# Attention and a gated mixer in one kernel: ScalarE units of two PSUM banks, spread weight loads, and an order planned with other durations

## The chip, the cores and the metric

The kernel runs on one core of a Trainium2 chip. The metric is the device time of one execution in microseconds (us); the time before is the median of three runs, 762.45 us (760.06 to 764.45). One further execution was profiled; where a single operation, a wait or a sum is spoken of, it is from that one.

## The reference

Two blocks read the same input x (2048 tokens, 512 wide, bfloat16), and a gate mixes them. Block A is attention with 32 heads of 16; block B is a small mixer with token shifts and a second MLP of width 1792.

```python
g = _sigmoid((x * gate_w).sum(-1, keepdims=True))
# block A
q, k, v = heads(x @ wqkv)                       # 32 heads of 16
p = softmax(einsum("bhqd,bhkd->bhqk", q, k) * 16 ** -0.5)
a = merge(einsum("bhqk,bhkd->bhqd", p, v)) @ wo
# block B
h = gelu(layernorm(x) @ w1)                     # its four quarters moved by 1, -1, 2, -2 tokens
x1 = x + shifted(h) @ w2
b = x1 + gelu(layernorm(x1) @ w3) @ w4
return g * a + (1 - g) * b
```

## The kernel before

**Score tiles.** Attention is cut into 32 rounds: four chunks of 512 queries (`c`), four groups of eight heads (`G`), and the two parities of heads (`p`). A round has 64 score tiles: 16 key tiles of 128 (`kt`) for four heads (`i`), each head on its own 32 rows of TensorE. In all there are 2048 score matmuls (`qk_op`, L1293), each 128 keys by 512 queries, each filling one of the eight PSUM banks. The planner counts its progress in these tiles.

**Two ways to the exponential.** `issue_act` gives two or three neighbouring banks to ScalarE as one unit: a single `Exp` instruction over all of them (L1388) writes `pa_all`. `issue_dve` gives a tile to VectorE instead: a multiply and add into 16-bit integers, which read as bfloat16 approximate the exponential (L1418, the first step, into `PD`). Two such tiles make a pair, and `close_pair` makes three shifted copies of the pair, by VectorE (L1456) or GpSimd (L1458). A ScalarE tile needs one matmul with V afterwards (`take_pv`, L1510), a VectorE tile needs four, one for each copy, which average the error away.

**TensorE's two tilings.** Score matmuls use four row tiles of 32 rows. All others that matter use four column tiles of 32 columns: the matmuls with V, and the weight matmuls of the projections and MLPs, which `gen` records (L975). So TensorE changes between groups of score matmuls and stretches of column passes. A pass here is one matmul on each of the four column tiles.

**Layer steps in between.** `mlp1` and `mlp2` are the mixer's two MLPs. `normalise` makes `xn` (L1142) of a chunk, writes it to DRAM, and reads it back transposed as `xnT`. The matmuls with `w1`, `w2`, `w3` and `w4` come from `gen` with a planned place (`at`) and a due place (`due`), both in score tiles. Five Gelu instructions on ScalarE (one at L1182, four at L1213) take a whole chunk or all of them, each between two loads of the activation table. At a round's end `finish_round` divides by the sums, through several small transfers.

**The order.** Nothing of the order is left to a scheduler of the framework. `Sim` plays the engines in Python while the kernel is built: each job has an engine, a planned duration (`hold`), a delay until its result can be used (`lat`), a priority and the buffers it takes. `pe_pick` decides what TensorE gets next, ahead of all a unit for ScalarE where the banks allow it; `try_engine` picks the job of lowest priority number of the other four queues. What the play starts first is issued first, engine by engine, and the chip then follows that order with its own durations. Where TensorE has nothing in the play for 250 ns, `filler` issues idle matmuls on zeros (L1819).

**The knobs.** `BASE` and `STEPS` set some 30 numbers of these decisions, and `STEPS` may change them at every 8 score tiles (`SEG = 8`). The ones that this text needs: `CAP2` and `CAP3` are the most banks that ScalarE's units may hold when a unit of two or of three banks is to be added (0 means never); `P1_PRIO` and `S_PRIO` are the priorities of VectorE's first step and of its copies, against 0.35 of `xn`; `GP2` and `GP3` share the copies out between VectorE and GpSimd; `DVE_STOP` and `DVE_WAIT` limit VectorE's tiles.

**Durations that the planner uses before.** A unit of w banks on ScalarE takes

```python
hold = 0.833 * 512 * w + 67.0
```

a weight load lands 6.0 us after its issue whatever its size, and a copy on GpSimd can begin when no other copy through the port it shares with VectorE is planned to run:

```python
if j.port and self.lock > self.t or j.acq and any(not self.fits(b) for b in j.acq):
    continue
```

The four loads of `w3` may be issued from score tile 450 of the planner's places on (`P_LD[0]`), the four of `w4` from 888 (`P_LD[1]`).

Of the kernel before, what the change touches and what calls it, by code (L numbers as in the profile page):

```python
# [97 lines left out]
class Job:  # L98
    __slots__ = ("eng", "hold", "lat", "deps", "prio", "fn", "acq", "frees", "at", "done", "start", "seq", "ready", "name", "port", "watch", "deps_tiles")

    def __init__(self, eng, hold, lat, deps, fn, prio=5, acq=(), frees=(), at=0, name="", port=False):
        self.port = port
        self.eng, self.hold, self.lat, self.deps, self.fn = eng, hold, lat, list(deps), fn
        self.prio, self.acq, self.frees, self.at = prio, list(acq), list(frees), at
        self.done = self.start = None
        self.seq = 0
        self.ready = None
        self.name = name
        self.watch = []

# [41 lines left out]
class Sim:  # L152
# [4 lines left out]
    def __init__(self, slots):  # L157
# [13 lines left out]
        self.lock = 0.0  # L171
        self.pending = 0
# [109 lines left out]
    def try_engine(self, e):  # L282
# [17 lines left out]
        j = best[1]  # L300
# [9 lines left out]
        if j.port:  # L310
            self.lock = self.t + j.hold
        self.busy[e] += j.hold
# [3 lines left out]
        self.push(self.t + j.hold + j.lat, lambda: self.finish_job(j))  # L316
# [60 lines left out]
def kernel(  # L377
# [14 lines left out]
    nc = tc.nc  # L392
# [60 lines left out]
    STEPS = {  # L453
        0: dict(DVE_STOP=8, SL0=165, AHEAD2=16, PV_IDLE=0.117, MAXU=4, LIMD=4, LIMA=2),
        1: dict(DVE_STOP=6, DVE_WAIT=1, AHEAD=16, PV_IDLE=0.5, MAXU=3, AT_SH=69, LIMD=3, LIMA=3),
        2: dict(P1_PRIO=0.743, GP2=0.5, DVE_STOP_L=16, DVE_WAIT=3, AHEAD=3, PV_IDLE=0.731, PRESS=15, DUE_SH=16, CAP2=6,
            RES=1, JOIN=1),
        3: dict(P1_PRIO=0.414, S_PRIO=0.3, DVE_STOP=13, DVE_STOP_L=14, EARLY=64, AHEAD=9, AHEAD2=24, PV_FULL=0.947,
            PRESS=18, CAP2=5, CAP3=6, RES=0),
        5: dict(S_PRIO=0.38, DVE_STOP=8, DVE_ALONE=-158, EARLY=99, AHEAD=3, PV_FULL=0.813, MAXU=9, ROT=1, AT_SH=96,  # L460
            HOLE=2),
        6: dict(MAXU=2),
        7: dict(GP2=0.315, URG_L=18, DVE_ALONE=2, AHEAD=9, PRESS=26, MAXU=3, CAP3=5),
        8: dict(URG_L=12, AHEAD=12, PV_FULL=0.916, PRESS=18, MAXU=4, AT_SH=69, HOLE=7, ACC2=1),
        9: dict(P1_PRIO=0.743, S_PRIO=0.625, EARLY=64, AHEAD=9, AHEAD2=13, PV_FULL=0.947, PV_IDLE=0.117, MAXU=5, ROT=3,
            HOLE=2, CAP3=6),
        10: dict(AHEAD=12, AHEAD2=24, LIMD=2),
        11: dict(URG_L=18),
        12: dict(P1_PRIO=0.279, GP2=0.655, URG_L=12, EARLY=99, AHEAD=9, AHEAD2=13, PV_FULL=0.916, MAXU=3, ROT=0, HOLE=3,
            LIMD=3, ACC2=0),  # L470
        13: dict(P1_PRIO=0.55, GP2=0.315, EARLY=64, IDLE_NS=700, DVE_WAIT=4, AHEAD2=5, MAXU=4, HOLE=7, MAXG=2),
        14: dict(P1_PRIO=0.743, URG_L=18, IDLE_NS=537, DVE_WAIT=3, AHEAD=12, AHEAD2=24, PV_FULL=0.947, MAXU=5, ROT=3,
            HOLE=2, MAXG=1, LIMD=2, ACC2=1),
        15: dict(DVE_WAIT=2),
        16: dict(URG_L=12, DVE_WAIT=3, AHEAD=9, HOLE=0, LIMD=3),
        17: dict(P1_PRIO=0.279, GP3=1, HOLE=2, MAXG=2),
        18: dict(P1_PRIO=0.743, GP3=0.967, EARLY=99, SL0=45, IDLE_NS=374, PD_LOW=3, AHEAD2=5, PV_FULL=0.916, HOLE=7,
            MAXG=1, CAP3=0, ACC2=0),
        19: dict(DVE_ALONE=-158, EARLY=64, SL1=0, IDLE_NS=459, AHEAD2=24, PV_IDLE=0.5, ROT=0),
        20: dict(URG=8, URG_L=18, SL1=60, IDLE_NS=374, PD_LOW=1, PV_FULL=0.97, PV_IDLE=0.117, HOLE=2),  # L480
        21: dict(URG=5, URG_L=12, SL1=0, IDLE_NS=459, PD_LOW=3, PV_FULL=0.916, PV_IDLE=0.5, HOLE=7),
        22: dict(HOLE=3),
        23: dict(DVE_STOP_L=12, HOLE=7),
        25: dict(DVE_STOP_L=14, URG=8, DVE_ALONE=2, IDLE_NS=864, PD_LOW=1, PA_LOW=3, AHEAD2=13, ROT=3, AT_SH=96, CAP2=6,
            LIMD=4, JOIN=0),
        26: dict(DVE_STOP=4, URG=5, URG_L=18, SL1=60, IDLE_NS=700, PD_LOW=3, PA_LOW=0, DVE_WAIT=4, AHEAD2=24,
            PV_IDLE=0.117, AT_SH=69, CAP2=5, LIMD=3, JOIN=1),
        27: dict(GP3=1, DVE_STOP=8, URG=8, EARLY=99, SL0=100, SL1=0, PD_LOW=2, DVE_WAIT=3, AHEAD=7, PV_FULL=0.947,
            PV_IDLE=0.5, HOLE=2, LIMA=2),
        28: dict(URG_L=12, SL0=45, IDLE_NS=374, AHEAD=9, DUE_SH=-6, HOLE=7, LIMA=3),  # L490
        29: dict(P1_PRIO=0.136, GP3=0.967, EARLY=64, IDLE_NS=864, AHEAD2=13, PV_FULL=0.916, PV_IDLE=0.731, DUE_SH=16,
            AT_SH=96, CAP2=6, LIMD=4, JOIN=0),
        30: dict(P1_PRIO=0.743, S_PRIO=0.178, GP2=1, DVE_STOP_L=16, URG=11, IDLE_NS=374, AHEAD2=24, PV_IDLE=0.5, ROT=0,
            AT_SH=69, CAP2=4, ACC2=1, JOIN=1),
        31: dict(S_PRIO=0.625, DVE_STOP_L=14, EARLY=99, PV_IDLE=0.731, ROT=3, CAP2=5, ACC2=0, JOIN=0),
        32: dict(DVE_STOP_L=16, EARLY=64, IDLE_NS=459, PA_LOW=1, PV_FULL=0.947, PV_IDLE=0.5, ROT=0, LIMA=4),
        33: dict(S_PRIO=0.178, DVE_STOP_L=7, URG=3, IDLE_NS=374, PA_LOW=0, AHEAD=12, PV_FULL=0.916, PRESS=11, ROT=2,
            AT_SH=118, ACC2=1, LIMA=3, JOIN=1),
        34: dict(S_PRIO=0.625, DVE_STOP_L=14, URG=11, IDLE_NS=864, PD_LOW=3, AHEAD=9, AHEAD2=9, PV_IDLE=0.117, PRESS=18,
            ROT=0, AT_SH=69, ACC2=0, JOIN=0),  # L500
        35: dict(SL1=60),
        36: dict(P1_PRIO=0.414, SL1=0, ACC2=1),
        37: dict(P1_PRIO=0.743, ACC2=0),
        38: dict(DVE_STOP_L=16, DVE_ALONE=-158, IDLE_NS=459, PD_LOW=2, PA_LOW=1, AHEAD2=24, PV_FULL=0.947, PRESS=57,
            MAXU=3, CAP3=5, LIMA=4),
        39: dict(P1_PRIO=0.55, S_PRIO=0.214, DVE_STOP_L=14, URG=2, DVE_ALONE=2, SL0=0, PD_LOW=3, AHEAD=5, PV_FULL=0.916,
            PRESS=18, MAXU=2, CAP2=4, CAP3=0, ACC2=1, LIMA=2, JOIN=1),
        40: dict(P1_PRIO=0.743, S_PRIO=0.625, URG=11, DVE_ALONE=-81, SL0=45, PD_LOW=2, AHEAD=9, PV_IDLE=0.5, PRESS=11,
            MAXU=5, ROT=1, ACC2=0, LIMA=4, JOIN=0),
        41: dict(SL0=165),  # L510
        42: dict(S_PRIO=0.214, GP3=0.8, SL0=45, AHEAD=7, PV_IDLE=0.117, PRESS=43, MAXU=4),
        43: dict(DVE_STOP_L=7, HOLE=3, CAP3=6),
        44: dict(SL1=60),
        45: dict(S_PRIO=0.178, DVE_STOP=6, DVE_STOP_L=12, DVE_ALONE=2, SL0=0, SL1=0, IDLE_NS=864, PV_FULL=0.947,
            PRESS=26, HOLE=2, CAP3=0, JOIN=1),
        46: dict(IDLE_NS=537, MAXG=2),
        49: dict(IDLE_NS=459, DUE_SH=32, MAXG=1),
        50: dict(JOIN=0),
        51: dict(S_PRIO=0.3, IDLE_NS=537, JOIN=1),
        52: dict(S_PRIO=0.178, IDLE_NS=459, MAXU=5, DUE_SH=16),  # L520
        53: dict(IDLE_NS=864, MAXU=4),
        54: dict(IDLE_NS=459, DUE_SH=32, LIMA=2),
        55: dict(PD_LOW=3, LIMA=4),
        56: dict(DVE_ALONE=138, PD_LOW=2, PA_LOW=0, JOIN=0),
        57: dict(DVE_STOP=4, DVE_STOP_L=14, URG=8, DVE_ALONE=362, EARLY=99, PD_LOW=3, PA_LOW=1, PV_FULL=0.97, DUE_SH=16,
            MAXG=2, ACC2=1),
        59: dict(DVE_STOP=6, DVE_STOP_L=12, URG=11, DVE_ALONE=2, EARLY=64, PD_LOW=2, PV_FULL=0.947, MAXU=5, MAXG=1,
            ACC2=0, JOIN=1),
        60: dict(DVE_STOP=4, DVE_STOP_L=14, URG=8, DVE_ALONE=362, EARLY=99, PD_LOW=3, PV_FULL=0.97, MAXU=4, ROT=2,
            MAXG=2, CAP2=6, CAP3=5, ACC2=1),  # L530
        61: dict(S_PRIO=0.625, GP3=0.967, DVE_STOP=13, DVE_STOP_L=16, PRESS=11, MAXU=7, HOLE=0, CAP3=0),
        62: dict(DVE_STOP=4, IDLE_NS=537, PV_FULL=0.916, PRESS=26, HOLE=3, MAXG=1),
# [1386 lines left out]
```

## Time and profile before

| what | value |
|---|---|
| median of three runs | 762.45 us |
| profiled execution | 761.38 us, span of its instructions 759.4 us |
| ScalarE busy | 735.6 us, 744 instructions |
| TensorE busy (matmuls) | 746.4 us, 9545 matmuls recorded |
| VectorE busy | 704.9 us, 1428 instructions |
| GpSimd busy | 460.4 us, 458 instructions |
| ScalarE's exponentials | 669 of two banks, 50 of three |
| transfers | 34.57 MB, 46 GB/s on average |

Busy time is the time in which an engine had at least one instruction running. Matmuls and ScalarE's instructions overlap with their neighbours, so the mean duration of one is longer than the spacing between two of them. Score tiles can be read off the trace by counting matmuls of L1293: number 1024 starts 380.6 us into the span, number 1152 at 424.7.

### The profile page before, as it was taken

The numbers are of one execution on the slowest core, as the hardware profiler recorded it, in microseconds if no ns is written. First come the engines' busy times: TensorE is split into PE (matmuls) and PEld (weight loads), VectorE is DVE, ScalarE is ACT, GpSimd is POOL, SyncE is SP. The second block draws the span as 40 slices with busy tenths as digits, with TensorE's granted clock in tenths as the row PEclk, the third lists the DMA queues.
The fourth block names the chain that finished last, engine by engine and source line by source line (L and its number), as shares of the span: only waits on it lengthen the run. The fifth ranks groups of instructions, "written<-read, shape, count | busy, mean of one in ns | idle before, by whom it ended". The sixth has DMA issues, their size and how long they took to land.

```text
span 759.4 us, 23495 instructions
## 1 busy us (share of the span) xinstructions
PE 746.4 (98%) x9545; PEld 218.2 (29%) x9545; DVE 704.9 (93%) x1428; ACT 735.6 (97%) x744; POOL 460.4 (61%) x458
## 2 busy tenths in 40 slices
PE   9999999999999999999999999999999999999997
PEld 5343222222322222223222222422223222222332
DVE  6999899999999999999998999898999999999966
ACT  6999999999999999999998999999999999999995
POOL 2334476776785456775645767465466577767732
PEclk9999999999999999999999999999999999999999
DMA  9433211231001320042101000202000001000001
GB/s 189 150 87 58 53 47 33 48 100 65 21 6 48 79 68 13 15 133 65 38 15 33 27 20 21 47 11 58 23 27 19 15 17 28 26 27 21 20 16 34
DMA packets 67091, 34.57 MB, mean 46 GB/s; under 512 B 46748, under 2 KB 62380, under 8 KB 66984
## 3 DMA queue, kind: packets, MB, share of 16 engines
q1 hardware_dynamic: 66040, 32.56, 17.6%
q8 instruction: 74, 1.21, 0.7%
q10 hardware_dynamic: 944, 0.52, 0.2%
q14 instruction: 33, 0.27, 0.1%
HBM read 17.40 MB, written 6.81 MB: 32 GB/s over the span
## 4 chain that ended last, share of the span: by engine, by line
PE 72%; ACT 10%; DVE 9%; issue 3%; DMA 2%; POOL 2%; SPq 1%; POOLq 0%; DVEq 0%; ACTq 0%
PE banks L1510 25%; PE banks L1293 25%; PE banks L975 21%; ACT pa_all L1388 10%; DVE PD L1418 4%; DVE PD L1456 3%; POOL PD L1458 2%; DMA oD<-oT 1%; DMA pk<-den 1%; DMA xn_dram<-xn 1%; PE banks L954 0%; PE banks L1840 0%; SPq L1550 0%; POOL oT L1546 0%; PE banks L996 0%
## 5 line engine op out<-in xcount | busy, mean ns | idle before, releaser
L1388 ACT ACTIVATE pa_all<-banks 128x1024 bf16<-128x1024 f32 x719 | 685.7, 1137 | 9.8 <-PE banks L1293 7.9
L1458 POOL TENSOR_SCALAR PD<-PD 128x1024 uint16<-128x1024 uint16 x396 | 407.7, 1051 | 255.0 <-DVE PD L1456 117.8
L1418 DVE TENSOR_SCALAR PD<-banks 128x512 uint16<-128x512 f32 x554 | 366.3, 685 | 27.9 <-PE banks L1293 24.1
L1510 PE MATMUL banks<-PD,V 128*17 128x512 bf16 (+1 forms) x2240 | 300.2, 382 | 3.3 <-DVE PD L1456 1.5
L1293 PE MATMUL banks<-q,kT 32*128 32x512 bf16 x2048 | 288.8, 384 | 2.5 <-ACT pa_all L1388 1.3
L1510 PE MATMUL banks<-pa_all,V 128*17 128x512 bf16 (+1 forms) x1488 | 269.3, 381 | 0.0
L1456 DVE TENSOR_SCALAR PD<-PD 128x1024 uint16<-128x1024 uint16 x444 | 192.0, 476 | 1.4
L1293 PEld LDWEIGHTS <-kT 32*128 32x128 bf16 x2048 | 72.5, 91 | 313.9 <-ACT pa_all L1388 296.0
L1510 PEld LDWEIGHTS <-V 128*17 128x17 bf16 (+1 forms) x3728 | 72.5, 88 | 122.5 <-issue 104.3
L975 PE MATMUL banks<-xnT,w 128*32 128x512 bf16 x1152 | 95.6, 383 | 0.4 <-DVE PD L1418 0.2
L975 PE MATMUL banks<-w,hT 128*32 128x512 bf16 x704 | 59.6, 382 | 0.0
L975 PEld LDWEIGHTS <-w 128*32 128x32 bf16 x1920 | 43.6, 95 | 45.6 <-issue 27.4
L1546 POOL TENSOR_TENSOR oT<-accsb,bcs 128x512 bf16<-128x512 f32 x31 | 39.5, 1275 | 25.2 <-DVE PD L1456 16.0
L975 PE MATMUL banks<-w,hB 128*32 128x512 bf16 x448 | 43.0, 383 | 0.0
L975 PE MATMUL banks<-w,w 128*32 128x256 bf16 (+1 forms) x768 | 41.3, 311 | 0.0
L975 PE MATMUL banks<-wo,oD 128*32 128x512 bf16 x224 | 29.9, 383 | 1.2 <-DMA oD<-oT 1.1
L1530 DVE COPY accsb<-banks 128x512 f32<-128x512 f32 x31 | 21.1, 679 | 3.6 <-PE banks L1510 3.0
L975 PE MATMUL banks<-w,wq 128*32 128x512 bf16 x256 | 22.8, 383 | 0.3 <-ACT w L1006 0.3
L975 PEld LDWEIGHTS <-hT 128*32 128x32 bf16 x704 | 16.6, 95 | 18.9 <-issue 12.1
L1122 DVE BATCH_NORM_STATS2 st<-x_sb 128x6 f32<-128x512 bf16 x32 | 21.6, 683 | 0.1
L1212 DVE CAST hB<-banks 128x512 bf16<-128x512 f32 x28 | 18.9, 680 | 1.5 <-PE banks L975 1.4
L1212 DVE CAST hT<-banks 128x512 bf16<-128x512 f32 x28 | 18.8, 680 | 0.8 <-PE banks L975 0.7
(90 smaller groups left out, 253.9 us busy)
## 6 DMA issues: line engine op xcount, KB each, us to landing
bcs<-rr SPq DMA_DIRECT2D x124, 64.0 KB
xn_dram<-xn SPq DMA_DIRECT2D x32, 128.0 KB
w<-in_B_w_dram SPq DMA_DIRECT2D x5, 512.0 KB
oD<-oT SPq DMA_DIRECT2D x124, 16.0 KB
w<-in_B_w_dram SPq DMA_DIRECT2D x4, 448.0 KB
out_dram<-ot SPq DMA_DIRECT2D x14, 128.0 KB
x_sb<-in_A_x_dram SPq DMA_DIRECT2D x3, 512.0 KB
w<-in_A_wqkv_dram SPq DMA_DIRECT2D x2, 256.0 KB
```

Source lines behind the costliest of these rows:

```text
L975: units.append([Op("col", j, lambda j=j, lf=lf, rf=rf, n0=n0, n1=n1, st=st, sp=sp: nc.tensor.matmul(get()[32 * j:32 * j + 32, n0:n1], lhsT ...
L1122: a = dve(600, deps, lambda: nc.vector.bn_stats(out=sb.slot[:], in_=x_sb[:, t, :]), prio=6, at=at, acq=[sb])
L1212: pre.append(evac(g, PSUM_NS, lambda ps, m=m: nc.vector.tensor_copy(out=h2()[:, m, :], in_=ps[:])))
L1293: o = Op("row", i, lambda: nc.tensor.matmul(dst(), lhsT=kT[G][32 * i:32 * i + 32, kt * P:(kt + 1) * P], rhs=qbuf[G, c].slot[32 * i:32 * i ...
L1388: job = act(hold, ops, lambda: nc.scalar.activation(out=pa_all[:, pb.cut(), :], in_=unit()[:, rb.cut(), :], func=ACT.Exp, scale=0.25), acq ...
L1418: return nc.vector.tensor_scalar(out=pr["buf"].slot[:].rearrange("p (b c) -> p b c", c=512)[:, h0:h0 + w, :], in0=unit()[:, rb.cut(), :], ...
L1456: return nc.vector.tensor_scalar(out=d[k][:, 0:w], in0=d[0][:, 0:w], scalar1=float(SHIFT * k), scalar2=None, op0=ALU.add)
L1458: return nc.gpsimd.tensor_scalar(out=d[k][:, 0:w], in0=d[0 if both else 2][:, 0:w], scalar1=1.0, scalar2=float(SHIFT * (k if both else 1)) ...
L1510: return nc.tensor.matmul(one(accs[r])[32 * i:32 * i + n, :], lhsT=lhs(n), rhs=rhs(), start=st and not edge, stop=True, tile_position=(0, ...
L1530: e = dve(PSUM_NS, round_ops[r], lambda: nc.vector.tensor_copy(out=ab.slot[:], in_=one(accs[r])), acq=[ab], prio=0, frees=[accs[r], Call(a ...
L1546: n = gp(1250, d3, lambda: nc.gpsimd.tensor_tensor(out=ob.slot[:], in0=ab.slot[:], in1=bb.slot[:], op=ALU.mult), acq=[ob], frees=[ab, bb], ...
```

## The change

ScalarE's units have two banks throughout: `CAP3` is 0 everywhere, and `CAP2` is 6, or 5 for a stretch. A new knob, `GATE`, lets units be issued only while ScalarE's units hold no more than that many banks. The planner's durations are others: ScalarE's fixed part is 55 ns, weight loads take a time that goes by their size through a common queue, other transfers on that queue land no earlier than it allows, and GpSimd's copies wait in the play until VectorE's last port operation has ended and its result has landed. The loads of `w3` and of `w4` are released 20 score tiles apart from each other. `STEPS` is another table throughout. The operations that make up one ScalarE unit of two banks, one VectorE tile or one weight matmul are the same as before; how many of each there are, and in which order they stand, follows from the play. Lines after L920 or so have lower numbers in the changed kernel, most of them by 72 (L1388 becomes L1316, L1819 becomes L1747).

```diff
 def try_engine(self, e):
 ...
-            if j.port and self.lock > self.t or j.acq and any(not self.fits(b) for b in j.acq):
+            if j.port and (self.lock > self.t or e == "POOL" and self.dve_lock > self.t) or j.acq and any(not self.fits(b) for b in j.acq):
                 continue
 ...
         if j.port:
             self.lock = self.t + j.hold
+            if e == "DVE":
+                self.dve_lock = self.t + j.hold + j.lat
 ...
-        self.push(self.t + j.hold + j.lat, lambda: self.finish_job(j))
+        end = self.t + j.hold + j.lat
+        if e == "SP" and j.hold > 1.5:
+            if j.size:
+                self.queue = max(self.queue, self.t + j.hold) + j.size / 185.0
+            end = max(end, self.queue + 1500.0)
+        self.push(end, lambda: self.finish_job(j))

 BASE
-        ROT=2, DUE_SH=-14, AT_SH=0, HOLE=7, MAXG=1, CAP2=4, CAP3=0, LIMD=3, RES=0, ACC2=0, LIMA=3, JOIN=0,
+        ROT=2, DUE_SH=-14, AT_SH=0, HOLE=7, MAXG=1, CAP2=6, CAP3=0, LIMD=3, RES=0, GATE=2, ACC2=0, LIMA=3, JOIN=0,

 STEPS (another table; two entries of each)
-        0: dict(DVE_STOP=8, SL0=165, AHEAD2=16, PV_IDLE=0.117, MAXU=4, LIMD=4, LIMA=2),
-        246: dict(P1_PRIO=0.414, DVE_STOP=13, DVE_ALONE=138, AT_SH=0, CAP3=5),
 ...
+        0: dict(P1_PRIO=0.55, S_PRIO=0.178, DVE_STOP_L=7, SL0=165, DVE_WAIT=4, PV_FULL=0.813, LIMD=4),
+        101: dict(PD_LOW=1, CAP2=5, GATE=4),
 ...
 def wload(name, src, users):
 ...
-        dl_w[name] = dma(6000.0, [], fn, acq=[wslot(name, users)], prio=2)
+        dl_w[name] = dma(4000.0, [], fn, acq=[wslot(name, users)], prio=2)
+        dl_w[name].size = 2 * src.shape[0] * src.shape[1]
 ...
-    dl_w["o"] = dma(5000.0, [], lambda: nc.sync.dma_start(out=wo[:], in_=wrows(A_wo)), prio=2)
+    dl_w["o"] = dma(4000.0, [], lambda: nc.sync.dma_start(out=wo[:], in_=wrows(A_wo)), prio=2)
+    dl_w["o"].size = 2 * D * D

 def issue_act(got):
 ...
-        hold = 0.833 * 512 * w + 67.0
+        hold = 0.833 * 512 * w + 55.0

 loads of w3 and w4
-        dl_w[f"3{i}"].at = P_LD[0]
+        dl_w[f"3{i}"].at = P_LD[0] + 20 * i
 ...
-        dl_w[f"4{i}"].at = P_LD[1]
+        dl_w[f"4{i}"].at = P_LD[1] + 20 * i

 def pe_pick():
 ...
-        for _ in range(2):
+        for _ in range(2 if act_banks[0] <= K.GATE else 0):
             free = len(sim.free["bank"])
             got = None
             for w, cap in ((3, K.CAP3), (2, K.CAP2)):
```

More of the change, by code (lines that the diff above doesn't have):

```diff
@@ L109, in __init__ @@
         self.watch = []
+        self.size = 0
 class Op:
@@ L171, in __init__ @@
         self.lock = 0.0
+        self.dve_lock = 0.0
+        self.queue = 0.0
         self.pending = 0
@@ L460 @@
[L460 to L466, printed above, removed]
@@ new lines @@
+        49: dict(MAXU=2),
+        50: dict(PV_FULL=0.86),
+        51: dict(PV_FULL=0.916),
+        52: dict(DVE_ALONE=500),
+        53: dict(DVE_STOP=8, PRESS=8),
+        54: dict(S_PRIO=0.178),
+        56: dict(HOLE=3),
+        57: dict(SL1=0),
+        59: dict(GP3=1),
+        60: dict(PV_FULL=0.86),
+        61: dict(PV_IDLE=0.5, AT_SH=118),
+        63: dict(P1_PRIO=0.279),
+        64: dict(PV_FULL=0.916),
+        65: dict(DVE_ALONE=-81, PV_IDLE=0.117),
+        66: dict(PRESS=15),
@@ new lines @@
+        200: dict(MAXU=3),
+        201: dict(DVE_STOP=6, ACC2=1),
+        202: dict(GP3=0.967),
+        203: dict(MAXG=1),
+        205: dict(GP3=0.9, MAXG=2),
+        207: dict(ROT=2),
+        209: dict(PRESS=43),
+        210: dict(SL0=0),
+        211: dict(P1_PRIO=0.55, SL1=0),
+        213: dict(PD_LOW=1),
+        214: dict(ROT=1),
+        215: dict(PD_LOW=2, ROT=2),
+        216: dict(MAXU=7, AT_SH=0),
+        219: dict(PV_FULL=0.813),
+        221: dict(DVE_ALONE=362),
+        223: dict(AT_SH=34),
@@ L746 @@
+        248: dict(DUE_SH=32),
+        249: dict(PA_LOW=3),
+        250: dict(ROT=3),
+        251: dict(PD_LOW=2),
+        254: dict(PD_LOW=1, ROT=1),
+        255: dict(DVE_ALONE=362, SL1=200, AT_SH=69),
     }
```

452 lines of the change are left out of this document (169 added, 283 removed).

## The prediction

> **What bounds the kernel now.** First the page, then the groups by form, then the order of time on ScalarE and on TensorE. The page says that three engines are nearly full, which doesn't say which of them sets the pace:
>
> ```profile
> PE 746.4 (98%) x9545; PEld 218.2 (29%) x9545; DVE 704.9 (93%) x1428; ACT 735.6 (97%) x744; POOL 460.4 (61%) x458
> PEclk9999999999999999999999999999999999999999
> ```
>
> TensorE's clock is full all along. The groups by form give ScalarE's two shapes of a unit, and the copies that a VectorE tile costs:
>
> ```profile
> L1388 ACT ACTIVATE pa_all<-banks 128x1024 bf16<-128x1024 f32 x669 | 628.5, 1106 | 9.7 <-PE banks L1293 7.9 <-PE banks L975 1.0 <-PE banks L1510 0.2
> L1388 ACT ACTIVATE pa_all<-banks 128x1536 bf16<-128x1536 f32 x50 | 77.2, 1543 | 0.1
> L1458 POOL TENSOR_SCALAR PD<-PD 128x1024 uint16<-128x1024 uint16 x396 | 407.7, 1051 | 255.0 <-DVE PD L1456 117.8 <-PE banks L1293 36.6 <-DVE PD L1418 30.1
> L1418 DVE TENSOR_SCALAR PD<-banks 128x512 uint16<-128x512 f32 x548 | 359.2, 679 | 27.7 <-PE banks L1293 23.8 <-POOL PD L1458 0.7
> L1456 DVE TENSOR_SCALAR PD<-PD 128x1024 uint16<-128x1024 uint16 x444 | 192.0, 476 | 1.4
> ```
>
> GpSimd idles 255 us: it doesn't bound. ScalarE in order of time, three rows of three windows (start, length, work):
>
> ```profile
> 10.30 5.62 ACT L1388 ACTIVATE pa_all<-banks 128x1024 bf16<-128x1024 f32 x6
> 378.39 14.02 ACT L1388 ACTIVATE pa_all<-banks 128x1024 bf16<-128x1024 f32 x15
> 741.38 9.23 ACT L1388 ACTIVATE pa_all<-banks 128x1024 bf16<-128x1024 f32 x9 [0.15 <-PE banks L1293]
> ```
>
> The mean of 1106 ns is no price, as neighbours overlap. In the middle row 15 units take 14.02 us, the last of them 1.106: (14.02 - 1.11) / 14 rounds to 0.92, and the same over the rows of the whole trace gives 0.917 us a unit. A third bank adds 1543 - 1106 = 437 ns: 1.35. The train of exponentials runs from 10.30 to 741.38 + 9.23 = 750.61, so 740.3 us. In it 669 x 0.917 + 50 x 1.35 = 681.0 are exponentials; 45.0 are the five Gelus (12.4 + 12.4 + 7.0), ten table loads (6.4 + 5.1 + 1.3) and one small operation (0.4). The 14.3 left over are all that ScalarE waits. ScalarE is thus the bound, and TensorE is close behind:
>
> ```profile
> 384.29 0.39 PE L1293 MATMUL banks<-q,kT 32*128 32x512 bf16 x3
> 384.62 0.61 PE L975 MATMUL banks<-w,hB 128*32 128x512 bf16 x8
> 385.16 0.39 PE L1293 MATMUL banks<-q,kT 32*128 32x512 bf16 x3
> 385.49 0.39 PE L975 MATMUL banks<-w,hB 128*32 128x512 bf16 x1
> ...
> 386.25 0.39 PE L1293 MATMUL banks<-q,kT 32*128 32x512 bf16 x2
> ```
>
> TensorE alternates between a group of score matmuls (L1293, row tiles) and passes of four column tiles (L1510, L975). A group and two passes take 0.87, a group and three 1.09: a pass costs 0.217, and the two changes of tiling 0.22 together. With two passes TensorE is 0.05 faster than ScalarE's unit, with three 0.17 slower: the 98% is mostly real.
>
> **The change, part by part.** All durations in the planner (the fixed 55 ns, GpSimd waiting for VectorE, the transfers' queue) are numbers in Python: they cost nothing themselves and act through the order. So I count the order in which the changed program's instructions stand.
>
> *ScalarE.* 758 units of two banks, none of three: 1516 score tiles, where there were 669 x 2 + 50 x 3 = 1488. 758 x 0.917 = 695.1 against 681.0: **+14.1 us** on the engine that is the bound, 28 tiles and 39 fixed parts. With Gelus and loads it needs 740.1 in the train. With the 10.3 ahead, the 8.8 behind (759.4 - 750.6) and no wait at all the span would be 759.2, that of before. All that remains is the waits.
>
> By the Trainium skill, page "ScalarE: Activation LUTs", section "What ACT_TABLE_LOAD costs", an ACTIVATE with immediate scale and bias takes 186 ns + 0.833 per element, and neighbours overlap by 93: 946 ns in series for two banks, 1373 for three, an estimate that would make it +15.5 us. The trace has 1106 alone and 917 in series; it decides. The page's rule speaks against this change: a fixed part that is paid more often.
>
> *VectorE and GpSimd.* 560 - 532 = 28 tiles fewer: VectorE loses 20 first steps of 0.655 (359.2 / 548), four double ones of 1.2 and eight copies of 0.43, 21 us together; GpSimd loses 34 copies of 1.03, 35 us. Neither is the bound, so I count no gain.
>
> *TensorE.* A VectorE tile needs four output matmuls (L1510), a ScalarE tile one: 28 x 3 = 84 fewer, 21 passes. But there are 739 groups of score matmuls where there were 721, 132 more fillers (33 short passes of 0.16), and more passes in which some of the four columns are empty. Summed over the order: 731 score passes and 1853 column passes before, 754 and 1923 after, times 0.217, plus 0.22 for each group: 717 and 741. **+24 us** on the second tightest engine, which was 14 below ScalarE's 731 (the whole of its work) and is now 4 below its 745. That is nothing while ScalarE is the longer of the two everywhere, so what counts is where the work lies.
>
> *Where it lies.* In the changed order, `normalise` of the second layer's first chunk stops after its third `xn` (L1142 of before) at score tile 676 and goes on at tile 1001; before, it and its transposes were through by tile 658. So the matmuls of `w3` start some 350 tiles later. Per 128 tiles, weight matmuls (L975) before and after, TensorE's sum and ScalarE's sum after:
>
> - tiles 768 to 895: 87 and 0; 37 against 42
> - tiles 896 to 1023: 236 and 32; 38 against 42
> - tiles 1024 to 1151: 188 and 452; 59.4 against 53.7 (49 units x 0.917, a Gelu of 6.18, two loads of 1.28)
> - tiles 1152 to 1279: 144 and 268; 49 against 45
>
> TensorE's slack in the first two is lost, and in the next two it is the bound. To price this I take in each stretch the larger of the two sums, and add up what lies over ScalarE's. How finely one cuts is a choice, as some two units in flight even out only short stretches. In stretches of 512 tiles the excess is 0.5 before and 14.2 after; of 128, 3.3 and 20.2; of 64, 12.2 and 24.8; of 32, 14.1 and 36.6; of 16, 16.9 and 43.8. Stretches of 32 give the 14.3 that before really waits, but some of that waits for transfers, so those of 64 are as near. The increase is 12.6 to 26.8; I take the mean of 64 and 32: **+17.5 us**.
>
> *Weight loads.* The `w3` loads stand at tiles 441 to 498 (before 434 to 443), those of `w4` at 882 to 935 (872 to 885); the four transposes of the next x, from 899 to 920, now stand among them on SP's queue, and their users come at tile 1000 or later. First use of `w3` is past tile 1023, of `w4` behind the Gelu at 1116: 180 tiles, some 60 us, hide the last load. Nothing; without that cover one late load would cost a few us once. The score gate (`GATE`) issues fewer units ahead; its cost is in the order already.
>
> *Sum.* The profiled execution is 761.4 (span 759.4 and 2.0 around it), 1.1 under the median of 762.45. 761.4 + 14.1 + 17.5 = 793, so some 794 against the median.
>
> **Rivals.** (1) *Only ScalarE's own work counts.* Waits stay at 14.3, because transfers and late operands made them and the order's mended durations remove as many as TensorE adds: 761.4 + 14.1 = 775.5. For it: the rows of ScalarE's waits are few (13 for score matmuls, 7.9 us). Against: the excess of 14 even in stretches of 512 tiles, which no two units in flight can bridge. (2) *The waits vanish: no change or faster.* The order then fits the chip so well that ScalarE never starves: 759.2 + 2.0 = 761.2, no change. Faster takes one thing more, a unit at 908 ns as the planner's new 55 ns say: 758 x 0.009 = 6.8 less, 754.4. It decides where the waits come under 4 us at 917 for no change, and under 3 us at 908 for faster. Against: no stretch of the trace has units below 916, the first projections and the `xn` transfers alone made ScalarE wait 3.9 us (idle of 0.79, 0.73, 0.53, 1.37 and 0.52 before score groups up to 90 us), and TensorE's sum rises. (3) *Worse: the holes don't overlap with anything.* The order has column sections of 5.1 us at tile 1074, 5.5 at 654 and 6.7 at 1178 with no Gelu beside them, where one or two queued units (0.9 to 1.8) cover little; if operands from GpSimd or the late `xn` chain hold TensorE inside them, stretches of 16 count and some more: 14.1 + 26.8 = 40.9 and up to 10, so 803 to 813.
>
> **How the numbers follow.** A measurement of this kernel can tell about 0.5% (3.8 us) from no change. Forecast (785 to 803): 0.60. Rival 1 and what lies between (766 to 785): 0.19. Rival 3 (over 803): 0.14. No change: 0.05. Faster: 0.02. So slower by over 0.5% has 0.93. The range from 773 to 808 leaves out the 0.07 of the last two, some 0.06 of rival 1 and 0.07 of rival 3: 0.20.
>
> **What would show it.** In the profile after: 758 units with a mean near 1106 ns and a spacing of 0.917; ScalarE busy 735.6 + 14 = 750, a share near 95%, with idle before L1388's exponentials up from 9.8 to over 20 us, released by TensorE; VectorE's busy time near 684, GpSimd's near 425; the stretch from score tile 1024 to 1151, 44 us before (380.6 to 424.7), at 59 or more; ScalarE full between tiles 768 and 1023. The prediction is wrong if the spacing is below 0.91, if ScalarE's waits stay under 15 us, or if they come from transfers.

## The result: 803.6 us, 5.4% slower, and the profile after

Four runs of the changed kernel have a median of 803.56 us (802.73 to 804.13); four of the kernel before 762.87 (760.06 to 764.45). The ratio is 1.0537 (1.0503 to 1.057). The profiled execution took 804.13 us, its span 802.4. First the page after, with the busy time of each engine and the rows of slices of ScalarE and of TensorE's clock:

```profile
PE 778.8 (97%) x9593; PEld 226.9 (28%) x9593; DVE 685.1 (85%) x1396; ACT 748.6 (93%) x783; POOL 426.1 (53%) x424
...
ACT  6999999999997999999787599999899999999995
...
PEclk9999999999999999999999999999999999999999
```

ScalarE works longer than before (735.6) and still has a smaller share. Between its ends its row has six slices below 9, of 20 us each: the 13th (from 241 us), the 20th to the 23rd (381 to 461 us) and the 29th (from 562 us). TensorE's clock is not the reason: its mean is 0.998 of full speed, with one stretch at half, 3.4 us long, from 372.1. The page's group of ScalarE's units, and the waits of ScalarE (the sum in us, the number of waits, the longest):

```profile
L1316 ACT ACTIVATE pa_all<-banks 128x1024 bf16<-128x1024 f32 x758 | 698.7, 1139 | 37.8 <-PE banks L1438 27.0
```

```profile
ACT pa_all L1316 <- PE banks L1438: 27.0, 10, 8.7
ACT pa_all L1316 <- PE banks L1221: 10.6, 9, 4.5
```

Before, 13 waits for score matmuls came to 7.9 us and none was over 1.4. Now few waits make the sum. ScalarE in order of time (start, length, work, idle before) shows the longest of them:

```profile
252.70 12.94 ACT L1316 ACTIVATE pa_all<-banks 128x1024 bf16<-128x1024 f32 x14 [4.54 <-PE banks L1221]
...
398.10 14.77 ACT L1316 ACTIVATE pa_all<-banks 128x1024 bf16<-128x1024 f32 x16 [4.28 <-PE banks L1438]
...
416.27 6.18 ACT L1141 ACTIVATE hB<-hB 128x7168 bf16<-128x7168 bf16 x1 [2.10 <-DVE hB L1140]
...
439.02 12.02 ACT L1316 ACTIVATE pa_all<-banks 128x1024 bf16<-128x1024 f32 x13 [3.44 <-PE banks L1438]
459.74 10.19 ACT L1316 ACTIVATE pa_all<-banks 128x1024 bf16<-128x1024 f32 x11 [8.70 <-PE banks L1438]
```

And TensorE in order of time, around 249, 394 and 455 us, shows what it does in three of them:

```profile
247.60 1.06 PE L903 MATMUL banks<-w,hT 128*32 128x512 bf16 x16
...
248.92 2.78 PE L903 MATMUL banks<-w,hT 128*32 128x512 bf16 x48
...
252.27 0.60 PE L1221 MATMUL banks<-q,kT 32*128 32x512 bf16 x5
...
393.88 0.39 PE L1221 MATMUL banks<-q,kT 32*128 32x512 bf16 x2
394.19 3.42 PE L903 MATMUL banks<-xnT,w 128*32 128x512 bf16 x60
...
452.44 1.96 PE L903 MATMUL banks<-w,hB 128*32 128x512 bf16 x29
454.32 0.39 PE L1221 MATMUL banks<-q,kT 32*128 32x512 bf16 x1
454.64 1.48 PE L903 MATMUL banks<-w,hB 128*32 128x512 bf16 x24
457.34 1.05 PE L903 MATMUL banks<-wo,oD 128*32 128x512 bf16 x16 [1.22 <-DMA oD<-oT]
459.24 0.61 PE L1438 MATMUL banks<-pa_all,V 128*32 128x512 bf16 x6 [0.85 <-DVE ot L1176]
```

Each time TensorE works through weight matmuls for 3.4 us and more, with no score group for ScalarE among them; the one matmul of L1221 at 454.32 is a single tile, and ScalarE's units have two. These are the places that the prediction named from the order: counted from 0, the next score matmuls after the sections are tiles 654 (at 252.27), 1074 (at 399.27) and 1179 (at 460.87), and the single one is 1178. ScalarE idles 4.5, 4.3 and 8.7 us there.

The time is put together in one sum, in which the waits are what is left of the train. It uses the spacing of 0.917 us, which holds after as well: 16 units take 14.77, and (14.77 - 1.02) / 15 = 0.917, where 1.02 is the row of a single unit. All in us:

| part of the profiled execution | before | after | change |
|---|---|---|---|
| ahead of the first exponential | 10.3 | 10.3 | 0 |
| exponentials, units x spacing | 681.0 | 695.1 | +14.1 |
| Gelus, table loads and the rest within the train | 45.0 | 45.0 | 0 |
| ScalarE's waits, what is left of the train (740.3 and 783.4) | 14.3 | 43.3 | +29.0 |
| behind the last exponential | 8.8 | 8.6 | -0.2 |
| around the span | 2.0 | 1.8 | -0.2 |
| sum | 761.4 | 804.1 | +42.7 |

By stage, tiles 1024 to 1151 took 66.2 us (44.1 before) and tiles 1152 to 1279 took 55.0 (42.1): +35.1 of the 42.9 by which the span grew. The other fourteen stages of 128 tiles differ from before by -6.1 to +8.7, and by 7.9 in all.

### The profile page after: what moved, and what is told of

Its sections match the earlier page's. It is cut to its first block, busy times and chain, and to the rows that moved or that the text cites. A ratio compares the mean times of both kernels' runs of the same rounds, so it can differ in the third digit from the quotient of the medians.

```text
span 802.4 us, 23537 instructions
## 1 busy us (share of the span) xinstructions
PE 778.8 (97%) x9593; PEld 226.9 (28%) x9593; DVE 685.1 (85%) x1396; ACT 748.6 (93%) x783; POOL 426.1 (53%) x424
## 3 DMA queue, kind: packets, MB, share of 16 engines
q1 hardware_dynamic: 66040, 32.56, 16.6%
## 4 chain that ended last, share of the span: by engine, by line
PE 56%; ACT 33%; issue 6%; DVE 3%; SPq 1%; DMA 1%; POOL 0%; ACTq 0%; POOLq 0%
ACT pa_all L1316 30%; PE banks L1221 19%; PE banks L1438 18%; PE banks L903 17%; DVE PD L1346 1%; ACT hT L1141 1%; SPq L1478 1%; ACT L1316 1%; DVE PD L1384 1%; PE banks L882 0%; DMA pk<-den 0%; PE banks L1768 0%; DMA oD<-oT 0%; DVE hB L1140 0%; ACT w L934 0%
## 5 line engine op out<-in xcount | busy, mean ns | idle before, releaser
L1316 ACT ACTIVATE pa_all<-banks 128x1024 bf16<-128x1024 f32 x758 | 698.7, 1139 | 37.8 <-PE banks L1438 27.0
L1386 POOL TENSOR_SCALAR PD<-PD 128x1024 uint16<-128x1024 uint16 x362 | 373.2, 1046 | 333.4 <-DVE PD L1384 141.5
L1346 DVE TENSOR_SCALAR PD<-banks 128x512 uint16<-128x512 f32 x530 | 352.1, 684 | 52.0 <-PE banks L1221 47.0
L1221 PE MATMUL banks<-q,kT 32*128 32x512 bf16 x2048 | 297.8, 385 | 11.7 <-ACT pa_all L1316 9.5
L1384 DVE TENSOR_SCALAR PD<-PD 128x1024 uint16<-128x1024 uint16 x436 | 184.2, 464 | 4.0 <-PE banks L1438 0.6
L1221 PEld LDWEIGHTS <-kT 32*128 32x128 bf16 x2048 | 75.0, 91 | 332.5 <-ACT pa_all L1316 294.4
L1438 PEld LDWEIGHTS <-V 128*17 128x17 bf16 (+1 forms) x3644 | 74.6, 88 | 129.4 <-issue 107.2
L903 PEld LDWEIGHTS <-w 128*32 128x32 bf16 x1920 | 45.5, 95 | 51.5 <-issue 26.0
L903 PE MATMUL banks<-w,hB 128*32 128x512 bf16 x448 | 41.8, 383 | 0.0
L903 PE MATMUL banks<-wo,oD 128*32 128x512 bf16 x224 | 34.5, 382 | 1.2 <-DMA oD<-oT 1.2
```

The source lines that it names most:

```text
L903: units.append([Op("col", j, lambda j=j, lf=lf, rf=rf, n0=n0, n1=n1, st=st, sp=sp: nc.tensor.matmul(get()[32 * j:32 * j + 32, n0:n1], lhsT ...
L1221: o = Op("row", i, lambda: nc.tensor.matmul(dst(), lhsT=kT[G][32 * i:32 * i + 32, kt * P:(kt + 1) * P], rhs=qbuf[G, c].slot[32 * i:32 * i ...
L1316: job = act(hold, ops, lambda: nc.scalar.activation(out=pa_all[:, pb.cut(), :], in_=unit()[:, rb.cut(), :], func=ACT.Exp, scale=0.25), acq ...
L1346: return nc.vector.tensor_scalar(out=pr["buf"].slot[:].rearrange("p (b c) -> p b c", c=512)[:, h0:h0 + w, :], in0=unit()[:, rb.cut(), :], ...
L1384: return nc.vector.tensor_scalar(out=d[k][:, 0:w], in0=d[0][:, 0:w], scalar1=float(SHIFT * k), scalar2=None, op0=ALU.add)
L1386: return nc.gpsimd.tensor_scalar(out=d[k][:, 0:w], in0=d[0 if both else 2][:, 0:w], scalar1=1.0, scalar2=float(SHIFT * (k if both else 1)) ...
```

## Experiments: what the units cost, and where the 29 us of waits come from

In the trace before, units of three banks end 1.344 us apart, so one bank more adds 0.427 us, and the fixed part of an instruction is 0.917 - 2 x 0.427 = 0.063. Most of ScalarE's +14.1 is thus the 28 more tiles, 12.0 us; the 39 more fixed parts make 2.5. (Together 14.4, since the sum above takes 1.35 for a unit of three banks, as the prediction did.) For the waits there were three theories: too much TensorE work in a stage; a wait for free slots of `pa_all`, since the waits end most often with a matmul with V; and the order itself, a table of knobs under which long weight sections stand where ScalarE has nothing in stock. In the kernels called "order fixed" the instructions stand as in the original but for the edit; in those called "planned anew" the plan makes another order. Beside the different runs the kernel before measured 761.3 to 762.9 us, so differences between runs of different experiments are good to a microsecond or two.

**One ScalarE instruction for each bank** (before, order fixed), to see the fixed part by itself and to see whether ScalarE is the bound.

```diff
-        job = act(hold, ops, lambda: nc.scalar.activation(out=pa_all[:, pb.cut(), :], in_=unit()[:, rb.cut(), :],
-                                                          func=ACT.Exp, scale=0.25), acq=[pb],
+        job = act(hold, ops, lambda: [nc.scalar.activation(out=pa_all[:, x.slot, :], in_=unit()[:, y.slot, :],
+                                                           func=ACT.Exp, scale=0.25) for x, y in zip(pb.bufs, rb.bufs)][-1], acq=[pb],
```

> The kernel before, order as it is, but each ScalarE unit is issued as one instruction per bank: 1488 instead of 719, 769 fixed parts more. By the spacing of the two forms (0.917 for two banks, 0.427 for a further one) the fixed part is 0.063 us: ScalarE's sum grows by 48, and if ScalarE is the bound the time goes to 797 (its 14 us of waits absorbed) to 810. If TensorE's order were the bound, ScalarE's extra work would hide in part: under 785. By the Trainium skill's page ScalarE: Activation LUTs the fixed part in series would be 93 ns: 71 us more, 819 to 833.

Measured: 799.8 us, 1.0493 times before (1.0463 to 1.0524). The page's group of ScalarE's units in this kernel:

```profile
L1388 ACT ACTIVATE pa_all<-banks 128x512 bf16<-128x512 f32 x1488 | 730.9, 870 | 3.5 <-PE banks L1293 2.4
```

A row of 21 in this kernel takes 10.39 us, 0.49 each, which is 0.427 + 0.063. There are 769 more instructions, so 48 us more work; the train grew by 39.0 (740.3 to 779.3), as the waits shrank from 14.3 to 5. So ScalarE sets the pace, a fixed part more costs 0.063 (with 0.093 it would have been the 819 us or more of the expectation's last sentence), and the waits of before are slack against TensorE that a longer ScalarE fills.

**Half of the weight matmuls** (order fixed). The second half of each accumulating group of `w1` to `w4` is left out, in the changed kernel and, as a control, in the one before. The edit is the same in both.

```diff
+            if not inst:
+                return
 ...
+            half = len(mms) // 2 if name in ("w1", "w2", "w3", "w4") else len(mms)
-            units.append([Op("col", j, lambda j=j, lf=lf, rf=rf, n0=n0, n1=n1, st=st, sp=sp: nc.tensor.matmul(
+            units.append([Op("col", j, lambda j=j, lf=lf, rf=rf, n0=n0, n1=n1, st=st, sp=i == half - 1 or sp, on=i < half: on and nc.tensor.matmul(
```

> The changed kernel with its order of instructions as it is, but of each weight matmul group of w1 to w4 only the first half of the contraction is done (the second half of the column passes is left out, with the products it would add). ScalarE, VectorE and GpSimd have the same instructions in the same order. Theory A (ScalarE starves where TensorE's column passes bunch up): TensorE's sum falls from 746 to 677 us, the excess over ScalarE in stretches of 32 score tiles from 39 to 10, so the 29 us of waits that the change added go: 770 to 778 us. Theory B (the added waits are for late operands and transfers, which stay as they are): 795 to 804 us.

> The kernel before with the same half of the weight matmuls left out. Theory A: the excess falls from 15 to 4 us in stretches of 32, so some 8 to 10 of its 14 us of waits go: 751 to 757 us. Theory B: the waits stay, 760 to 763 us. In both the difference to the changed kernel with halves is ScalarE's own 14 us and what is left of waits.

Measured: 802.51 us after, against 803.56 with all matmuls; 757.23 before, 0.9944 times its own (0.9926 to 0.9962), 0.2 us above theory A's range there. The waits left in the train are 9.7 us before (14.3 with all matmuls) and 40.6 after (43.3). The number after is in the range of theory B. The holes at the three long sections do shrink: 8.7 to 4.5 us, 4.5 to 4.3, 4.3 to 3.0. Something not expected took part of that back: TensorE's clock fell. The windows around the end of the first Gelu, in the changed kernel and then in this one (the columns are the stretch, its length, each engine's busy time with its instructions, TensorE's granted clock, the share of the DMA engines, GB/s):

```profile
222.00:231.00 9.00, 8.69 (x103) 2.17 (x97) 6.83 (x15) 9.00 (x11) 3.65 (x4) 1.00 0.01 2
```

```profile
222.00:231.00 9.00, 8.82 (x51) 1.70 (x51) 4.27 (x9) 7.08 (x8) 1.63 (x2) 0.50 0.02 3
231.00:240.00 9.00, 8.31 (x94) 2.07 (x92) 6.91 (x16) 8.12 (x9) 5.96 (x7) 0.93 0.02 3
```

At half the clock TensorE looks as busy with 51 matmuls as with 103, and ScalarE waits. The mean granted clock of the whole run is 0.982, and 1.8% of 799.6 us is 14 us of lost clock. But even if all 14 came back, 788 us would lie outside theory A's 770 to 778. And of ScalarE's 34.3 us of waits for TensorE here only some 6 to 8 stand within or close behind the stretches of low clock. TensorE's waits for ScalarE's banks, in the changed kernel and then in this one, show where much of the freed time went:

```profile
PE banks L1221 <- ACT pa_all L1316: 9.5, 34, 1.3
```

```profile
PE banks L1224 <- ACT pa_all L1319: 41.5, 120, 2.1
```

Between the sections TensorE now waits for ScalarE, and in the sections there are other things than weight matmuls: at tile 654, where the hole hardly shrank, TensorE waits 0.37 us for VectorE and 0.46 for GpSimd. So the sum of TensorE's work doesn't tell the waits of this run: the expectation counted 10 us of excess in stretches of 32 tiles, and 40.6 were waited. It shows that shorter sections make shorter holes; what the weight matmuls are worth at full clock it doesn't show.

**No fillers** (after, order fixed): the 208 idle matmuls of `filler` are left out.

```diff
-        ops = [Op("col", i, lambda i=i: nc.tensor.matmul(one(accs[r])[32 * i:32 * i + DH + 1, 0:384], lhsT=zero[:, 0:DH + 1], rhs=zero[:],
+        ops = [Op("col", i, lambda i=i: None and nc.tensor.matmul(one(accs[r])[32 * i:32 * i + DH + 1, 0:384], lhsT=zero[:, 0:DH + 1], rhs=zero[:],
```

> The changed kernel, order as it is, without the 208 filler matmuls on zeros (52 passes of 0.16, 8.5 us of TensorE's sum). Theory A: they stand where TensorE has slack or a Gelu runs beside them, and the excess in stretches of 32 falls by 1.2 us only: 801 to 803.5 us. Rival: they lie on the path with their whole length: 795 us. Second rival: without them TensorE idles, the clock drops, and it gets slower, over 805 us.

Measured: 806.43 us (804.76 to 811.51), 2.9 more than with fillers, in the range of the second rival. The long holes are the same to 0.1 us. Around the first Gelu the clock fell again. The changed kernel, then two windows of this one:

```profile
214.00:222.00 8.00, 6.46 (x115) 2.76 (x109) 4.81 (x10) 7.97 (x6) 4.00 (x4) 1.00 0.01 2
```

```profile
214.00:222.00 8.00, 4.81 (x31) 0.92 (x29) 4.28 (x8) 7.53 (x6) 3.63 (x4) 0.62 0.01 2
222.00:231.00 9.00, 8.88 (x80) 1.97 (x78) 4.99 (x12) 7.57 (x9) 2.09 (x2) 0.77 0.01 2
```

So leaving the fillers out shortens none of the long holes: no cost shows for the 132 additional ones, which the prediction counted as TensorE work. Without any, the clock falls.

**Exponentials written in place** (order fixed): ScalarE writes its result back into the PSUM banks, and `pa_all` is filled once at the start, so that no unit waits for a slot of it. The values that V is multiplied with are then constants. The same edit in the kernel before is the control.

```diff
+    sim.emit(2500.0, lambda: nc.vector.memset(pa_all[:], 1.0))
-        job = act(hold, ops, lambda: nc.scalar.activation(out=pa_all[:, pb.cut(), :], in_=unit()[:, rb.cut(), :],
+        job = act(hold, ops, lambda: nc.scalar.activation(out=unit()[:, rb.cut(), :], in_=unit()[:, rb.cut(), :],
```

> Control for the next run: the kernel before, order as it is, but each exponential is written back into its own PSUM banks and not into pa_all, which is filled with ones once (by VectorE, in the first microseconds); the matmuls with V read those. So no exponential waits until a matmul with V has read its slot of pa_all. The kernel before has 0.2 us of such waits: 758 to 766 us, the difference being the fill and what writing to PSUM costs or saves on ScalarE.

> The changed kernel, order as it is, with the same edit: exponentials written back into their PSUM banks, pa_all filled once. In the profile of the changed kernel 27.0 of ScalarE's 37.8 us of idle time before exponentials ended with a matmul with V (a slot of pa_all came free). Theory C1 (the full slots are themselves the limit): those 27 us go, some 775 us after the control's own shift. Theory C2 (the slots only show where TensorE's fixed order has no score group for ScalarE for several microseconds): each of the ten waits shortens by one queued unit at most, 0.9 us, and the rest then ends with a score group: 794 to 803 us after the control's own shift.

Measured: the control 766.57 us, 1.0077 times before (1.0055 to 1.0098), with a train that starts 5.5 us later behind the memset (15.8 where it was 10.3) and is no longer (739.2); the changed kernel 809.24, with a start at 16.6 and a train of 782.8 where it had 783.4. No gain. The control lies 0.6 us above its expected range and is 5.3 us slower than the kernel before. With that shift, theory C1 asked for some 780 us and C2 for 799 to 808; 809.24 is 1 us above C2. ScalarE's waits and three rows in order of time, in this last kernel:

```profile
ACT banks L1317 <- PE banks L1222: 36.5, 20, 8.5
```

```profile
406.46 13.04 ACT L1317 ACTIVATE banks<-banks 128x1024 f32<-128x1024 f32 x14 [4.11 <-PE banks L1222]
...
446.95 12.12 ACT L1317 ACTIVATE banks<-banks 128x1024 f32<-128x1024 f32 x13 [3.44 <-PE banks L1222]
...
467.59 2.84 ACT L1317 ACTIVATE banks<-banks 128x1024 f32<-128x1024 f32 x3 [8.51 <-PE banks L1222]
```

The same holes of 4.1, 3.4 and 8.5 us now end with a score group (L1222 here). The matmul with V was only the last of several things behind one section. The theory of the slots falls.

**One knob of the table** (after, planned anew): `S_PRIO` at segment 54. It is 0.178 from tile 432 to tile 992, so that VectorE's copies go ahead of `xn` (0.35); here 0.38 puts them behind it.

```diff
-        54: dict(S_PRIO=0.178),
+        54: dict(S_PRIO=0.38),
```

> The changed kernel planned again with one knob undone: at score tile 432 S_PRIO stays 0.38 and is not 0.178, so that VectorE's copies don't stand ahead of xn (0.35) up to tile 992. In the new order the second layer's first chunk is normalised by tile 640 (1001 in the changed kernel), the first Gelu of that layer is at tile 897 (1116). 755 units (758), TensorE's sum 736 (746), excess in stretches of 32 tiles 20 (39), of 16 tiles 36 (45). Theory A with the hold-up as the main cause: ScalarE 2.7 us less, excess 9 to 18 less: 783 to 792 us. Rival (the bunching comes from two-bank units and from the durations, whatever xn does): 798 to 804 us.

Measured: 789.04 us, 1.0356 times before (1.0338 to 1.0373). It is in the range of theory A. The train is 769.9 with 755 units, which leaves 32.6 us of waits where there were 43.3. So ending the hold-up of `xn` that the prediction saw was worth 14.5 us together with what else moved, 10.7 of them waits: over a third of the 29 added, not all.

**Three single changes of the plan** (planned anew), each alone. Before, without units of three banks; before, with the new rule for GpSimd's copies (`dve_lock`) only; after, with a fixed part of 55.5 ns instead of 55.

```diff
-            for w, cap in ((3, K.CAP3), (2, K.CAP2)):
+            for w, cap in ((2, K.CAP2),):
```

```diff
-            if j.port and self.lock > self.t or j.acq and any(not self.fits(b) for b in j.acq):
+            if j.port and (self.lock > self.t or e == "POOL" and self.dve_lock > self.t) or j.acq and any(not self.fits(b) for b in j.acq):
 ...
+            if e == "DVE":
+                self.dve_lock = self.t + j.hold + j.lat
```

```diff
-        hold = 0.833 * 512 * w + 55.0
+        hold = 0.833 * 512 * w + 55.5
```

> The kernel before, planned again with its own table and durations, but with no units of three banks. New order: 747 units, 554 VectorE tiles, TensorE's sum 749 (721 before), ScalarE's 731 (726), excess in stretches of 16 tiles 55 (18). Theory A (the price is the order: whatever changes a number of the planner loses what the table of knobs was fitted to): 731 + 55 + 17 = about 800, 788 to 806. Rival (two-bank units cost their own 4.4 us of ScalarE): 764 to 770.

> The kernel before, planned again with one of the changed durations only: GpSimd's copies wait until VectorE's last port operation has landed. New order: 677 units of two and 56 of three banks, 526 VectorE tiles (560), ScalarE's sum 742 (726), TensorE's 741, excess in stretches of 16 tiles 20. Theory A: 742 + 20 + 17 = 779, 772 to 784, nearly all by ScalarE's own work, since the planner now holds the way over VectorE and GpSimd for dearer. Rival (the mended duration makes the order fit the chip better, so that waits go): under 765.

> A control for what any new plan does: the changed kernel with ScalarE's fixed part at 55.5 ns instead of 55.0 in the planner, nothing else. New order: xn of the second layer's first chunk goes through at tiles 614 to 623 (663 to 1001), its first Gelu stands at tile 876 (1116). 754 units, ScalarE's sum 737 (741), TensorE's 748 (746), excess in stretches of 16 tiles 48 (45), of 32 tiles 37 (39). Theory A with the hold-up as one hole among several that an unfitted table leaves: 798 to 806, no better than the changed kernel. Rival (the hold-up is the cause of the slowdown): 780 to 790.

Measured: 791.77, 789.7 and 806.39 us, which is 1.0392 (1.0358 to 1.0426), 1.036 (1.0336 to 1.0384) and 1.058 (1.0547 to 1.0613) times before. The first is in its first theory's range. The second is 5.7 us above the upper end of its own: ScalarE's own work is 15.4 us more, as expected, and the waits are 28.0 where an excess of 20 was counted. The third, 0.4 us above its first theory's range, is the telling one: half a nanosecond in the plan made another order in which `xn` is not held up, and yet there are 51 us of waits, one of them twice as long as any of the changed kernel's:

```profile
ACT pa_all L1316 <- PE banks L1221: 28.0, 17, 17.9
ACT pa_all L1316 <- PE banks L1438: 18.9, 5, 7.6
```

The profile is of the slowest of its four runs (809.15 us), in which TensorE's clock was at half for 17 us, so a few of the 51 belong to the clock. Each of the three changes to the plan, even the one without meaning, gave another order, with 28 to 51 us of waits. So none of these runs gives the price of its one edit by itself.

**Other knobs under the changed plan** (planned anew). The changed kernel with its code, its durations and its units of two banks; 1694 values of the knobs at 248 of the segments are set anew, chosen by what TensorE has beside ScalarE's work in the plan. As a counterpart the same was tried with the kernel before.

```diff
+    TUNED = {
+        6: dict(PD_LOW=2),
+        8: dict(URG=3, EARLY=64),
 ...
+    for _n, _d in TUNED.items():
+        STEPS[_n] = {**STEPS.get(_n, {}), **_d}
     K = SimpleNamespace(**BASE)
```

> The changed kernel with all its code and durations, units of two banks only, and other values of the knobs from segment 6 on, chosen in the plan so that TensorE's sections lie beside ScalarE's work. ScalarE's own work stays that of the changed kernel: 757 units (758 there), 757 x 0.917 + 45 of Gelus and table loads. In the order, TensorE's sum over ScalarE's in stretches of 16 score tiles falls from 44.8 us to 15.5 (17.8 in the kernel before), xn of the second layer is through by tile 972 instead of 1089. Theory (the waits are this table's order, ScalarE's +14 is the price of the units): waits of 14 to 24 us, so 773 to 785 us. Rival (the holes belong to two-bank units and to durations that do not meet the chip's, whatever the table): waits of 38 or more, 797 to 808 us.

> The kernel before with other values of the knobs, chosen in the plan so that TensorE's excess over ScalarE in stretches of 16 tiles falls from 17.8 us to 13.3; units 679 of two banks and 44 of three, ScalarE's own work +1.1 us; the plan's own end is 3.0 us later than that of the kernel before. If the excess in stretches is what ScalarE waits for: 761.5 + 1.1 - 4.5, so 756 to 760 us. Rival (the plan's play, which has the transfers in it too, tells the end): 763 to 767 us.

Measured: 777.95 us, 1.0216 times before (1.0201 to 1.0231), and 764.53, 1.0048 times (1.0033 to 1.0063). The page of the first, and its waits:

```profile
PE 762.9 (98%) x9547; PEld 218.6 (28%) x9547; DVE 679.4 (87%) x1396; ACT 747.4 (96%) x782; POOL 430.0 (55%) x427
```

```profile
ACT pa_all L1568 <- PE banks L1690: 10.1, 6, 5.4
ACT pa_all L1568 <- PE banks L1473: 5.0, 8, 1.9
```

The work of ScalarE is that of the changed kernel (747.4 us, 757 units), and 25.6 us are gone, 24.8 of them waits: the train is 757.7, less 694.2 and 45.0 leaves 18.5. So neither units of two banks nor the mended durations make the holes; the order that the table gives does. (It also gives TensorE less to do: 762.9 us busy where it was 778.8.) What stays against before, 17.1 us of span, is 13.2 of ScalarE's work (694.2 - 681.0) and 4.2 of waits, less 0.3 at the two ends. The counterpart shows where such fitting ends: the order's excess fell by 4.5 us, the waits did not (15.9), ScalarE has 1.0 more to do, and it came out as the rival said. No version that beats the kernel before was found.

All orders with all their matmuls, with TensorE's excess over ScalarE in stretches of 16 score tiles, counted alike for all (this count gives 17.8 and 44.8 where the prediction had 16.9 and 43.8), and the waits left in the train:

| order | excess in the order, us | waits measured, us |
|---|---|---|
| before, other knobs | 13.3 | 15.9 |
| after, other knobs | 15.5 | 18.5 |
| before | 17.8 | 14.3 |
| before, new rule for GpSimd's copies | 20 | 28.0 |
| after, `S_PRIO` 0.38 | 36 | 32.6 |
| after | 44.8 | 43.3 |
| after, 55.5 ns | 48 | 51.1 |
| before, no units of three | 55 | 41.8 |

Six of eight agree within 4 us. The order with the new rule waits 8 us more than its excess; TensorE waits there 5.2 us for transposed `xn`, which no count of work contains. The one without units of three waits 13 less, and that stays open. The changed kernel with half of the weight matmuls fits least (10 in stretches of 32, 40.6 waited), so the count is a guide for whole orders and not the cause itself.

## Why the prediction was right in its mechanism and low in one term

*The bound and ScalarE's term.* ScalarE is the bound, the spacing is 0.917, and 758 units cost +14.1: shown by the sum above, and by the run with one instruction for each bank. ScalarE's busy time was forecast at 750 and is 748.6. The mean of one unit is 1139 ns where 1106 was forecast; as the spacing did not change, that says again that the mean is no price. The prediction broke this itself in two small places: it priced a third bank by a difference of means, 437 ns where the spacings give 427 (0.3 us in all), and called 1106 ns a unit alone, where a single one takes 1.02 us.

*The waits: the term that was mis-sized.* They were put at +17.5 and are +29.0. The step that failed is the choice of stretch. The mean of stretches of 64 and of 32 tiles was taken because stretches of 32 gave the 14.3 us that before waits. For stretches of 64, 32 and 16 tiles the kernel before hardly distinguishes the cuts (12.2, 14.1, 16.9), so that agreement chose nothing; after, the same cuts lie between 24.8 and 43.8. Stretches of 16 gave +26.8 and would have made 761.4 + 14.1 + 26.8 = 802.3 of the profiled execution, which took 804.1. With the mean that was taken the forecast was 794, and the measured 803.56 lies half a microsecond above its range of 785 to 803. What the rows show fits this: a section of 3.4 us and more outlasts ScalarE's stock, at most three units of 0.917 (`CAP2` is 6 banks), so work doesn't even out over more than a few units, and a stretch of 64 tiles (some 24 units) lets it. That 16 came so near is partly luck, since in the other orders the same count misses by up to 13 us.

*Which rival.* The size is that of rival 3, at its lower end, and its three places are the places of three of the largest holes, 17.5 us together. Its condition, operands that hold TensorE inside the sections, was needed for one of them at most: TensorE waited 1.2 us for `oD` and 0.9 for VectorE in the hole of 8.7, and for nothing in the rows shown at 249 and 394. Rival 1 (waits as before) failed by the 29 us. Rival 2 failed by the spacing, which did not follow the planner's 55 ns.

*The stages.* Tiles 1024 to 1151 were put at 59 us or more and took 66.2; the next 128 took 55.0 where TensorE's sum was 49. In both, the longer engine's sum is passed by 6 to 7 us, as the holes of one half were not made good in the other. ScalarE was full between tiles 768 and 1023 as forecast: 41.4 and 43.3 us, with no hole over half a microsecond.

*Terms at nothing.* VectorE (685.1, forecast 684) and GpSimd (426.1, forecast 425) gave no gain, and no late weight load is among the waits. TensorE's +24 us of work has no term of its own in the sum; what it cost is within the waits.

*The hold-up of `xn`.* It was told as the cause of the late `w3` matmuls. It is part of the slowdown: one knob against it gave 14.5 us back. But an order without it, that of 55.5 ns, was as slow as the changed kernel. The cause that the runs bear out is wider: the order that the table of knobs gives, since other knobs under the same plan take 24.8 of the 43.3 us of waits away. That the changed table was fitted to other numbers of the plan would explain it, but no run shows it.

## What to carry to other kernels

When an order is written out ahead, the sum of the work says whether it can be fast; the excess in short stretches (here 16 tiles, some six units) says more, within 4 us in six of eight orders. Choose that length by what the bounding engine can have in stock, not from an agreement in a kernel where all lengths give the same, and look at the sections themselves. And when knobs are fitted to a planner, mending the planner's durations without fitting them again can cost more than it brings: one mended rule alone made the kernel before 28 us slower, and other knobs gave 25.6 us back to the changed one. Judge the two apart.

## What the runs showed of the hardware that was not expected

*Less matmul work can halve TensorE's clock.* In the windows above the granted clock is 1.00 in the changed kernel, 0.50 with half of the weight matmuls (222 to 231 us), and 0.62 and 0.77 without fillers, each time around the end of the first Gelu, while nothing but TensorE's work was taken out. The Trainium skill, page "TensorE: Matmul & The Clock Gate", Part 1, says that the clock is gated by recent activity, half rate after an idle window of about 3.4 us. The 0.50 agrees with half rate; a longer window at 0.62 is a mean over both. The idle window does not show here: in the 10 us ahead of these falls TensorE's longest idle time is 1.5 us. The changed kernel itself ran at half from 372.1 to 375.5 us (0.79 in the window from 370 to 378) with no idle time over 0.21 us in the 10 us ahead. Until TensorE's last work, the stretches at half in these three runs last 3.4, 6.8 or 10.2 us, one, two or three times 3.41. That fillers of 0.16 us a pass prevent the fall around the first Gelu is shown by the run without them, which was 2.9 us slower.

*The name behind a wait can mislead.* 27.0 of the 37.8 us ended by the profile with matmuls with V. With that dependency gone, the same holes ended with score groups. A long hole is better read from what TensorE did in it than from what came last.

*ScalarE's fixed part* is 0.063 us in series: 0.490 a piece at 512 elements, 0.917 at 1024 and 1.344 at 1536 lie on one line with 0.427 for each 512.
